# A cosformer attention and token/channel mixer on one core: four tokens per partition, shared tails, a ones column, bf16 transposes, and attention emitted one batch ahead

## The chip, the cores and the metric

The kernel runs on one core of a Trainium2 chip. The metric is device time in microseconds (us), smaller is better. A program on one core has no second core to compare with; every run that is used here was classed as fast (within 1.5% of the fastest run of the same kernel). Engine names in the profile: PE is TensorE, DVE is VectorE, ACT is ScalarE, POOL is GpSimd, SP is SyncE, and PEld is the loading of weights into PE.

## The reference

There are 8 batches of 8 heads, 576 tokens and 64 features per head. Inputs are f32. Shortened:

```python
# attention: linear, with relu features weighted by cos and sin of the position
q_p = concat(relu(q) * cos_w, relu(q) * sin_w)         # [..., 576, 128]
k_p = concat(relu(k) * cos_w, relu(k) * sin_w)
kv  = einsum('bhsf,bhsd->bhfd', k_p, v)
z   = sum(k_p, axis=tokens)
num = einsum('bhsf,bhfd->bhsd', q_p, kv)
den = einsum('bhsf,bhf->bhs', q_p, z) + 1e-6
x   = num / den                                        # heads joined: [8, 576, 512]

# mixer: first over tokens (576 -> 256 -> 576), then over channels (512 -> 1536 -> 512)
u   = x + (relu(x^T @ w_tok1) @ w_tok2)^T
out = u + relu(u @ w_ch1) @ w_ch2
```

576 is four and a half times 128, the number of partitions. How the odd half (the last 64 tokens, "the tail") is treated is a large part of this case.

## The kernel before

Each batch is cut into five tiles of tokens: four of 128 and one of 64. Letters in the text name PE's stages: kv, z, num, den as in the reference, tr (transposes of q features), b (x times w_tok1), u, the transposes of u, c (w_ch1) and o (w_ch2).

```python
for b in range(B):
    for ci, (o, sz) in enumerate(s_sizes):          # 128, 128, 128, 128, 64
        nc.sync.dma_start(out=qt[:sz], in_=q[b, :, o:o + sz, :].rearrange("h s d -> s h d"))
        nc.sync.dma_start(out=kt[:sz], in_=...)      # rows of 64 f32 = 256 bytes
        nc.gpsimd.dma_start(out=vt[:sz], in_=...)    # converts to bf16 on the way
        # [cut: qp on ACT, kp on DVE]
        for h in range(H):
            nc.tensor.matmul(kv_ps[:F, h * D:(h + 1) * D], kph, vt[:sz, h, :], ...)
            nc.tensor.matmul(z_ps[:F, h:h + 1], kph, ones[:sz, :], ...)
        # [cut: transposes of qp, copied by ACT into qpT]
    for ci, (o, sz) in enumerate(s_sizes):
        for h in range(H):
            nc.tensor.matmul(num_ps[:sz, h * D:(h + 1) * D], lw, kv_sb[:F, h * D:(h + 1) * D], ...)
            nc.tensor.matmul(den_ps[:sz, h:h + 1], lw, z_sb[:F, h:h + 1], ...)
        nc.vector.tensor_scalar_add(den_sb[:sz, :], den_ps[:sz, :], 1e-6)
        nc.vector.reciprocal(den_sb[:sz, :], den_sb[:sz, :])
        nc.vector.tensor_mul(x_sb[:sz, ci, :], num_v, den_b[:sz])     # 128 x 512
    # [cut: b and B1]
    for ci, (o, sz) in enumerate(s_sizes):
        # [cut: two u matmuls] 
        nc.vector.tensor_add(u_sb[:sz, ci, :], u_ps[:sz, :], x_sb[:sz, ci, :])   # f32
    for ci, (o, sz) in enumerate(s_sizes):
        for cj in range(NCC):
            nc.tensor.transpose(t_ps[:P, cj, :sz], u_sb[:sz, ci, cj * P:(cj + 1) * P],
                                ident_f[:sz, :sz])                               # f32
        nc.scalar.copy(uT[:, :, o:o + sz], t_ps[:, :, :sz])
    for mi in range(NCH):
        for (no, nsz) in [(0, 512), (512, 64)]:      # c: a matmul of 512 columns, one of 64
            for ki in range(NCC):
                nc.tensor.matmul(c_ps[:, no:no + nsz], w_ch1[...], uT[:, ki, no:no + nsz], ...)
        # [cut: relu, ACT and DVE in turn]
    for ci, (o, sz) in enumerate(s_sizes):           # o: five tiles, the fifth of 64 rows
        # [cut: twelve o matmuls, add of u, store]
```

## Time and profile before

| what | value | where it is read |
|---|---|---|
| time | 416.13 us, median of 4 runs (414.42 to 417.54) | the runs |
| span of the profiled execution | 415.3 us | the page |
| start, until the c stage of batch 0 | 69.2 us | PE's timeline |
| one batch, c stage to c stage, mean of 7 | 45.3 us | PE's timeline |
| last c and o stages, then the last add and store | 25.2 + 3.9 us | PE's timeline |

The last three rows give the sum 69.2 + 7 x 45.3 + 25.2 + 3.9 = 415.4, the span up to rounding.

From the page of the kernel before, part 1 (busy us, share of the span, instructions), part 2 (the span in 40 slices, busy tenths; PEclk is the granted PE clock in tenths) and part 4 (the chain of work that ended last):

```profile
PE 352.4 (85%) x3168; PEld 201.4 (48%) x3168; DVE 161.3 (39%) x332; ACT 162.6 (39%) x283; POOL 62.7 (15%) x72
...
PE   0005178998999999998999899998999899999996
...
PEclk9999559998799989998999979998999899998999
DMA  9999983029901393029702791029402900110002
...
PE 76%; DMA 7%; SPq 6%; DVE 5%; ACT 5%; issue 1%; DVEq 0%; ACTq 0%
```

PE is what the span hangs on: 85% busy, and 76% of the chain. Two things are to be seen in the slices. The first seven (each 10.4 us) belong to the start, where DMA is full and PE has little to do at first. After them the row is nines with an eight in every fourth or fifth place, and PEclk has dips there too: once per batch PE has a weak stretch.

PE's waits before, from the table of waits (engine, line, releaser: us in total, times, longest):

```profile
PE z_ps L133 <- DVE kp L124: 28.1, 4, 14.7
PE den_ps L156 <- DVE den_sb L159: 15.8, 14, 9.1
PE z_ps L133 <- DVE kp L122: 6.4, 1, 6.4
```

The long ones among them (the longest are 14.7, 9.1 and 6.4 us) lie in the start. PE's timeline over one steady batch (start, duration, engine, line, operation, output and inputs, count, and in brackets the idle time just before and what ended it):

```profile
186.02 0.41 PE L131 MATMUL kv_ps<-vt,kp 128*128 128x64 bf16 x8
...
190.19 0.34 PE L156 MATMUL den_ps<-z_sb,qpT 128*128 128x1 bf16 x8 [0.26 <-DVE den_sb L159]
...
192.25 0.24 PE L156 MATMUL den_ps<-z_sb,qpT 128*128 128x1 bf16 x4 [0.53 <-DVE den_sb L159]
...
196.12 2.76 PE L171 MATMUL b_ps<-x_sb,w_tok_118 128*128 128x512 bf16 x10
198.81 1.23 PE L133 MATMUL z_ps<-ones,kp 128*128 128x1 bf16 x40
199.98 2.79 PE L179 MATMUL u_ps<-B_2221,w_tok_124 128*128 128x512 bf16 x10
202.78 2.81 PE L187 MATMUL t_ps<-ident_f,u_sb 128*128 128x128 f32 x20
205.93 12.14 PE L197 MATMUL c_ps<-uT,w_ch_127 128*128 128x512 bf16 x96 [0.34 <-ACT uT L189]
217.91 2.75 PE L210 MATMUL o_ps_2409<-w_ch_132,h1T 128*128 128x512 bf16 x12
```

The stages follow one another: attention (186.0 to 205.9), then c (12.1 us) as one block, then o. No c matmul stands inside the attention part, so nothing fills PE's short waits there.

### The profile page before, as it was taken

The numbers are of one execution on the slowest core, as the hardware profiler recorded it, in microseconds if no ns is written. First come the engines' busy times: TensorE is split into PE (matmuls) and PEld (weight loads), VectorE is DVE, ScalarE is ACT, GpSimd is POOL, SyncE is SP. The second block draws the span as 40 slices with busy tenths as digits, with TensorE's granted clock in tenths as the row PEclk, the third lists the DMA queues.
The fourth block names the chain that finished last, engine by engine and source line by source line (L and its number), as shares of the span: only waits on it lengthen the run. The fifth ranks groups of instructions, "written<-read, shape, count | busy, mean of one in ns | idle before, by whom it ended". The sixth has DMA issues, their size and how long they took to land.

```text
span 415.3 us, 7475 instructions
## 1 busy us (share of the span) xinstructions
PE 352.4 (85%) x3168; PEld 201.4 (48%) x3168; DVE 161.3 (39%) x332; ACT 162.6 (39%) x283; POOL 62.7 (15%) x72
## 2 busy tenths in 40 slices
PE   0005178998999999998999899998999899999996
PEld 0004154547454555447554655456554755465542
DVE  2002253327422554328332653346332743326231
ACT  4115164208531384209630664128520873051410
POOL 7363000006000320006000600024000600000000
PEclk9999559998799989998999979998999899998999
DMA  9999983029901393029702791029402900110002
GB/s 183 205 192 182 169 151 77 2 86 156 161 2 42 98 187 76 0 103 169 130 2 76 137 165 25 25 91 196 91 0 86 85 5 0 52 65 0 2 25 90
DMA packets 121043, 37.26 MB, mean 90 GB/s; under 512 B 113521, under 2 KB 115889, under 8 KB 121009
## 3 DMA queue, kind: packets, MB, share of 16 engines
q1 hardware_dynamic: 80256, 28.32, 30.7%
q0 software_dynamic: 40752, 8.46, 23.0%
q8 instruction: 25, 0.41, 0.5%
q14 instruction: 10, 0.07, 0.1%
HBM read 35.78 MB, written 9.44 MB: 109 GB/s over the span
## 4 chain that ended last, share of the span: by engine, by line
PE 76%; DMA 7%; SPq 6%; DVE 5%; ACT 5%; issue 1%; DVEq 0%; ACTq 0%
PE c_ps L197 23%; DMA kt<-in_k_dram 7%; PE b_ps L171 6%; PE num_ps L154 4%; PE tr_ps L141 4%; PE u_ps L179 4%; ACT uT L189 3%; SPq L113 3%; PE kv_ps L131 3%; SPq L112 3%; PE t_ps L187 3%; PE den_ps L156 2%; PE z_ps L133 2%; DVE kp L124 2%; DVE u_sb L181 1%; DVE kp L122 1%
## 5 line engine op out<-in xcount | busy, mean ns | idle before, releaser
L197 PE MATMUL c_ps<-uT,w_ch_127 128*128 128x512 bf16 (+1 forms) x768 | 97.0, 286 | 2.6 <-ACT uT L189 2.6
L114 POOL DMA_DIRECT2D vt<-in_v_dram x40 | 49.2, 1242 | 257.1 <-PE tr_ps L141 247.3
L142 ACT COPY qpT<-tr_ps 128x512 bf16<-128x512 bf16 (+1 forms) x80 | 40.4, 544 | 111.8 <-PE tr_ps L141 111.1
L197 PEld LDWEIGHTS <-w_ch_127 128*128 128x128 bf16 x768 | 51.0, 97 | 48.8 <-issue 2.5
L210 PEld LDWEIGHTS <-h1T 128*128 128x128 bf16 (+1 forms) x480 | 46.9, 100 | 55.3 <-issue 3.4
L205 DVE TENSOR_SCALAR h1T<-c_ps 128x576 bf16<-128x576 f32 x48 | 36.4, 758 | 83.2 <-PE c_ps L197 83.2
L203 ACT ACTIVATE h1T<-c_ps 128x576 bf16<-128x576 f32 x48 | 31.2, 650 | 61.4 <-PE c_ps L197 60.4
L120 ACT ACTIVATE qp<-qt,bias_112,cos_t 128x512 bf16<-128x512 f32 (+1 forms) x40 | 32.2, 805 | 23.1 <-DMA qt<-in_q_dram 23.1
L133 PE MATMUL z_ps<-ones,kp 128*128 128x1 bf16 (+1 forms) x320 | 10.5, 164 | 34.5 <-DVE kp L124 28.1
L181 DVE TENSOR_TENSOR u_sb<-u_ps,x_sb 128x512 f32<-128x512 f32 (+1 forms) x40 | 24.6, 681 | 30.0 <-PE u_ps L179 30.0
L122 DVE TENSOR_SCALAR kp<-kt,cos_t 128x512 bf16<-128x512 f32 (+1 forms) x40 | 19.9, 498 | 39.9 <-DMA kt<-in_k_dram 35.6
L156 PE MATMUL den_ps<-z_sb,qpT 128*128 128x1 bf16 (+1 forms) x320 | 18.5, 169 | 18.0 <-DVE den_sb L159 15.8
L121 ACT ACTIVATE qp<-qt,bias_112,sin_t 128x512 bf16<-128x512 f32 (+1 forms) x40 | 32.2, 804 | 1.7 <-DMA qt<-in_q_dram 1.7
L141 PE MATMUL tr_ps<-ident,qp 128*128 128x128 bf16 (+1 forms) x320 | 30.4, 221 | 0.7
L189 ACT CAST uT<-t_ps 128x512 bf16<-128x512 f32 (+1 forms) x40 | 20.1, 548 | 21.1 <-PE t_ps L187 20.1
L133 PEld LDWEIGHTS <-kp 128*128 128x128 bf16 (+1 forms) x320 | 9.4, 96 | 37.8 <-DVE kp L124 28.4
L164 DVE TENSOR_TENSOR x_sb<-num_ps,den_sb 128x512 bf16<-128x512 f32 (+1 forms) x40 | 25.3, 683 | 5.6 <-PE num_ps L154 4.9
L171 PE MATMUL b_ps<-x_sb,w_tok_118 128*128 128x512 bf16 (+1 forms) x80 | 26.7, 486 | 0.0
L156 PEld LDWEIGHTS <-qpT 128*128 128x128 bf16 (+1 forms) x320 | 16.0, 104 | 21.1 <-issue 17.9
L124 DVE TENSOR_SCALAR kp<-kt,sin_t 128x512 bf16<-128x512 f32 (+1 forms) x40 | 21.4, 535 | 3.3 <-DMA kt<-in_k_dram 3.3
L187 PE MATMUL t_ps<-ident_f,u_sb 128*128 128x128 f32 (+1 forms) x160 | 21.8, 273 | 0.9
L141 PEld LDWEIGHTS <-qp 128*128 128x128 bf16 (+1 forms) x320 | 20.8, 100 | 3.3 <-issue 0.2
(127 smaller groups left out, 307.3 us busy)
## 6 DMA issues: line engine op xcount, KB each, us to landing
qt<-in_q_dram SPq DMA_DIRECT2D x32, 256.0 KB, 6.5
kt<-in_k_dram SPq DMA_DIRECT2D x32, 256.0 KB, 5.5
out_dram<-res SPq DMA_DIRECT2D x32, 256.0 KB, 2.0
vt<-in_v_dram POOLq DMA_DIRECT2D x32, 128.0 KB, 6.9
w_ch_127<-in_moe_w_ch_dram POOLq DMA_DIRECT2D x4, 384.0 KB, 10.0
w_ch_132<-in_moe_w_ch_dram POOLq DMA_DIRECT2D x12, 128.0 KB, 8.4
qt<-in_q_dram SPq DMA_DIRECT2D x8, 128.0 KB, 3.9
kt<-in_k_dram SPq DMA_DIRECT2D x8, 128.0 KB, 3.5
```

What stands on the lines that cost most here:

```text
L114: nc.gpsimd.dma_start(out=vt[:sz], in_=v[b, :, o:o + sz, :].rearrange("h s d -> s h d"))
L120: nc.scalar.activation(qp[:sz, :, 0, :], qt[:sz], AF.Relu, bias=bias0[:sz], scale=c_s)
L121: nc.scalar.activation(qp[:sz, :, 1, :], qt[:sz], AF.Relu, bias=bias0[:sz], scale=s_s)
L141: nc.tensor.transpose(tr_ps[:F, hh, :sz], qph, ident[:sz, :sz])
L142: nc.scalar.copy(qpT[:F, g * HH:(g + 1) * HH, o:o + sz], tr_ps[:F, :, :sz])
L156: nc.tensor.matmul(den_ps[:sz, h:h + 1], lw, z_sb[:F, h:h + 1], start=True, stop=True)
L171: nc.tensor.matmul(b1_ps, w_tok1[:sz, ci, mi * P:(mi + 1) * P], x_sb[:sz, ci, :], start=(ci == 0), stop=(ci == NSC - 1))
L187: nc.tensor.transpose(t_ps[:P, cj, :sz], u_sb[:sz, ci, cj * P:(cj + 1) * P], ident_f[:sz, :sz])
L189: nc.scalar.copy(uT[:, :, o:o + sz], t_ps[:, :, :sz])
L197: nc.tensor.matmul(c_ps[:, no:no + nsz], w_ch1[:, ki, mi * P:(mi + 1) * P], uT[:, ki, no:no + nsz], start=(ki == 0), stop=(ki == NCC - 1))
L205: nc.vector.tensor_relu(h1T[:, mi, :], c_ps)
L210: nc.tensor.matmul(o_ps[:sz, :], h1T[:, ki, o:o + sz], w_ch2[:, ki, :], start=(ki == 0), stop=(ki == NCH - 1))
```

## The change

The intent is less PE work, and long DMA rows. Six things happen at once:

1. Four consecutive tokens lie in one partition, so that q, k and v come in rows of 1 KB instead of 256 bytes, and the first 512 tokens are four full tiles.
2. The 64-token tails of two batches share one 128-row tile for their features. Their u is kept, and the c and o stages of all eight tails run at the end as one group of 512 tokens. The c and o stages of a batch then have 512 tokens and no odd half.
3. A column of ones beside v makes kv and z one matmul of 65 columns; num and den likewise. The 80 matmuls of one column go. A PSUM tile now holds four heads, so that the normalisation is ten chains of 256 columns instead of five of 512.
4. POOL casts u to bf16, and u is transposed in bf16, eight blocks to a PSUM tile, with one ACT copy.
5. v is loaded as f32 and cast by POOL.
6. `attention(b)` and `channel_batch(b)` are functions, and attention is emitted ahead of the channel stages of the batch before it.

Lesser things change too: o has PSUM buffers of its own (before, it shared three with the attention), v comes over SP's queue, and the input tiles have other numbers of buffers. The core of the diff, with unchanged and lesser parts cut:

```diff
+    def load(b):
+        for t, src in ((kt, k), (vt, v), (qt, q)):
+            nc.sync.dma_start(out=t, in_=src[b, :, :SF, :].rearrange("h (p j) d -> p h (j d)", j=J))
 # [cut: load_tail: two batches' tails, one in each half of the partitions]
-                nc.tensor.matmul(kv_ps[:F, h * D:(h + 1) * D], kph, vt[:sz, h, :], ...)
-                nc.tensor.matmul(z_ps[:F, h:h + 1], kph, ones[:sz, :], ...)
+                    lhs, rhs = kp[:, j, h], vb[:, j, h, :D + 1]          # the last column is ones
+                    nc.tensor.matmul(kv_ps[:, hh, :], lhs.rearrange("p f d -> p (f d)"), rhs, ...)
-                nc.tensor.matmul(num_ps[:sz, h * D:(h + 1) * D], lw, kv_sb[...], ...)
-                nc.tensor.matmul(den_ps[:sz, h:h + 1], lw, z_sb[:F, h:h + 1], ...)
+        for j in range(J + 1):
+            for g in range(2):                                           # four heads each
+                    nc.tensor.matmul(nm[r0:r1, hh, :], lw, kv[:, h, :D + 1], start=True, stop=True)
+                nc.vector.tensor_scalar_add(den[r0:r1], nm[r0:r1, :, D:], 1e-6)
+                nc.vector.reciprocal(den[r0:r1], den[r0:r1])
+                nc.vector.tensor_mul(dst[r0:r1, g * HH:(g + 1) * HH], nm[r0:r1, :, :D], den_b[r0:r1])
-                nc.tensor.transpose(t_ps[:P, cj, :sz], u_sb[:sz, ci, ...], ident_f[:sz, :sz])
+            nc.gpsimd.tensor_copy(ub[:, j, :], u[:, j, :])               # f32 to bf16
+            if j % 2:
+                transposed(uT[:, j - 1:j + 1]..., ub[:, j - 1:j + 1]..., 2 * NCC)
+    attention(0)
+    attention(1)
+    for b in range(2, B):
+        load(b)
+        if b % 2 == 0:
+            load_tail(b // 2)
+        channel_batch(b - 2)
+        attention(b)
+    channel_batch(B - 2)
+    channel_batch(B - 1)
+    channel_tail()
```

The framework orders each engine's instructions at build time. In the built program, the attention of batch b stands among the c matmuls of batch b-1. I call such a kernel woven, and one whose stages follow one another unwoven.

## The prediction

> **What bounds the kernel now.** TensorE. The page has it busy 352.4 of 415.3 us, DVE and ACT 39% each; the chain that ended last is 76% PE. In PE's timeline a steady batch repeats every 45.05 us (first kv matmul at 186.02, the next at 231.07): attention with its stalls 10.1, b 2.7, z 1.2, u 2.8, transposes of u 3.1, c 12.1, o 13.0. Before that lies the start: c of batch 0 begins only near 70 us, with PE in long waits for kp and den (28.1 and 15.8 us in the table of waits), while DMA moves about 200 GB/s in 256-byte rows.
>
> **PE work after, per batch, from spacings in this trace.** A 512-column matmul follows the next after 0.216 us (12 in 2.59), a 65-column one after about 0.03, a bf16 transpose after 0.055 (4 in 0.22), an f32 one after 0.14 (20 in 2.80).
> - c: the 64-column matmuls go (12.14 to 10.4); o: the 64-row fifth tile goes (13.07 to 10.4). All tails return as a ninth group, 20.7 us in all, 2.6 per batch.
> - u transposes: 20 f32 become 18 bf16: -1.8.
> - z and den (80 small matmuls): about -2.5.
> - Sum: tr 2.0, kv 1.2, nm 1.4, b 2.2, u 2.2, tr(u) 1.0, c and o 20.7: 31; with the tails 33.4, so 268 for eight batches.
>
> **What it adds.** POOL casts about nine 128x512 f32 tiles per batch, in the path of v and of u. The trace has no such cast. The Trainium skill, "GPSIMD Engine Reference", section 3.1, gives 1.8 cycles per element at best, 768 ns for 512; my estimate is 0.8 to 1.3 us. It also says (section 1) that POOL shares SBUF interfaces with DVE; this trace cannot show it. DVE's normalisation becomes ten chains of add, reciprocal, multiply (0.16+0.20+about 0.42) instead of five (0.16+0.20+0.68): +2.6 us per batch. DVE rises to about 23 us per batch, ACT to 20: under PE's 33, but not inside the attention part.
>
> **How they stand in order.** The built order weaves attention of batch b into the c matmuls of batch b-1 and leaves o pure. The woven part is a chain: transposes with 1.0 us ACT copies (6 us to the first nm), ten DVE chains and two relus (9), b and B1 (3), u, cast, transpose, copy (6 to 7): about 25 us for 20.6 us of PE work. So 4 to 5 us of PE stalls per batch; a batch costs 35 to 36 us instead of 45.
>
> **Start.** Rows become 1 KB, but load 0 with its tail (3.9 MB) shares the engines with 7.5 MB of weights. PE's first instruction transposes the q tail, the last of these loads: about 33 us. Then an unwoven attention of 25: c of batch 0 starts near 58.
>
> **Sum.** 58 + 7 x 35.5 + 41.5 (c, o of the last batch and of the tails, nothing woven) + 4 (last add, store) = 352 us. Range 330 to 376. Faster by over 2%: 0.98; within: 0.015; slower: 0.005.
>
> **What the profile would show.** Right: 432 matmuls of 128x512 each in c and o at 0.216; period 35 to 36; PE waits for DVE, ACT copies and casts, each some tenths; first PE work near 33 us; last 41.5 us pure c and o. Wrong: period near 32, or above 38.
>
> **What would make it wrong.** Faster: stalls under 2 us per batch (320 to 330), or a start at over 300 GB/s (10 us less). Slower: casts over 1.5 us, or slowed by DVE; SP's in-order queue holding loads behind stores; a lower granted clock; strided reads of k or of w2's weights costing more than dense ones.

## The result, and the profile after

The kernel after takes 342.11 us (median of 4 runs, 340.8 to 344.09), the kernel before 416.13 us. The ratio is 0.821, with a 95% interval of 0.8165 to 0.8256. Ratios are the mean time of one kernel's fast runs over that of the other's of the same rounds, so not quite the ratio of the medians quoted. The output is correct.

| part of the span | before | after | difference |
|---|---|---|---|
| start, until the first c stage or the first woven stretch | 69.2 | 59.7 | -9.5 |
| seven periods | 7 x 45.3 | 7 x 33.3 | -84 |
| c and o with nothing woven in, at the end | 25.2 | 41.5 (batch 7, then the tails) | +16.3 |
| last add and store | 3.9 | 4.7 | +0.8 |
| span | 415.3 | 339.0 | -76.3 |

Nearly all of it comes from the period; part is given back at the end, as the tails' c and o move there. The page after, the same lines as before:

```profile
PE 286.0 (84%) x2076; PEld 146.5 (43%) x2096; DVE 166.3 (49%) x449; ACT 148.2 (44%) x217; POOL 54.3 (16%) x93
...
PE   0000567989999999999999999999999999999994
...
PEclk9999969999999999999999999999999999999999
DMA  7999999909747512832263110011002000301114
...
PE 61%; DVE 15%; SPq 8%; ACT 7%; issue 3%; POOL 2%; DMA 2%; POOLq 0%; DVEq 0%; ACTq 0%
```

PE's share of the span has not changed (84% for 85%), though its work fell by 66 us: a share says nothing of how much work there is. The weak stretches and the dips of the clock are gone from the slices. The chain has moved: 15% of it is DVE now, and POOL appears. PE's waits after:

```profile
PE tr L154 <- ACT qpt L143: 37.3, 1, 37.3
...
PE nm L223 <- DVE x L229: 3.3, 5, 1.5
...
PE tr L154 <- POOL ub L248: 2.9, 5, 1.2
```

One wait, that for the first transpose, is the start. All waits for the normalisation and for the casts come to 6.2 us in the whole span. PE's timeline of one woven stretch and of the pure o stage after it:

```profile
126.36 1.50 PE L154 MATMUL tr<-ident,qp 128*128 128x128 bf16 x24
...
131.32 0.55 PE L223 MATMUL nm<-kv,qpT 128*128 128x65 bf16 x12
...
133.39 0.30 PE L223 MATMUL nm<-kv,qpT 128*128 128x65 bf16 x4 [0.44 <-DVE x L229]
133.53 0.59 PE L271 MATMUL c_ps<-uT,wc_128 128*128 128x512 bf16 x2
133.96 0.29 PE L223 MATMUL nm<-kv,qpT 128*128 128x65 bf16 x4
134.09 0.59 PE L271 MATMUL c_ps<-uT,wc_128 128*128 128x512 bf16 x2
...
137.38 1.04 PE L236 MATMUL b_1458<-x,w_121 128*128 128x512 bf16 x4
...
140.57 1.03 PE L246 MATMUL u_ps<-B_1457,w_126 128*128 128x512 bf16 x4
...
150.15 9.88 PE L281 MATMUL o_ps<-wc_133,h_1542 128*128 128x512 bf16 x45
159.86 0.61 PE L154 MATMUL tr<-ident,qpt 128*128 128x128 bf16 x8
```

Read the nm rows against the c rows between them. Every 0.56 us there are four nm matmuls and two c matmuls, with no idle time in brackets. DVE meanwhile runs one chain. Its timeline in the same stretch shows at what pace:

```profile
133.99 0.42 DVE L229 TENSOR_TENSOR x<-nm,den 128x256 bf16<-128x256 f32 x1
134.33 0.17 DVE L226 RECIPROCAL den<-den 128x4 f32<-128x4 f32 x1
134.42 0.13 DVE L225 TENSOR_SCALAR den<-nm 128x4 f32<-128x4 f32 x1
134.53 0.42 DVE L229 TENSOR_TENSOR x<-nm,den 128x256 bf16<-128x256 f32 x1
```

The records of one chain sum to 0.42 + 0.17 + 0.13 = 0.72 us, but from one multiply to the next only 0.54 us pass: each record begins before the one ahead of it has ended (the reciprocal at 134.33, when the multiply that began at 133.99 has 0.08 us to run). So DVE at 0.54 and PE at 0.56 are level here, and the c matmuls hide the chains but for the 0.44 us of the first.

Busy times of one steady period each (the window's bounds, its length, then busy time and instructions of each engine, granted clock, DMA share and GB/s); the first line is of before, and the second fence is of after:

```profile
172.85:217.91 45.06, 43.35 (x402) 24.87 (x400) 20.07 (x41) 20.00 (x35) 6.72 (x5) 0.96 0.56 93
```

```profile
159.86:193.30 33.44, 32.66 (x250) 16.73 (x252) 19.08 (x53) 18.54 (x27) 5.25 (x8) 1.00 0.37 127
```

In both, PE (the first figure after the length) fills the period nearly, while DVE and ACT have about 20 us or less. PE's busy time includes the modelled ends of its records and, in before, some work at a lower clock (0.96), so it is more than the work at full clock. For that work this text uses two estimates: 30.8 us per period after, which is the number of matmuls of each kind times the usual spacing of that kind in the trace, and 39.9 us before, which is the sum of the stages in the expectation of experiment 2. They are not made in the same way: counted as the first is, the old operations come to 37.6 us (in the trace of experiment 2).

### The profile page after: what moved, and what is told of

Same layout as the page of the kernel before. It is cut to its first block, busy times and chain, and to the rows that moved or that the text cites. A ratio compares the mean times of both kernels' runs of the same rounds, so it can differ in the third digit from the quotient of the medians.

```text
span 339.0 us, 5197 instructions
## 1 busy us (share of the span) xinstructions
PE 286.0 (84%) x2076; PEld 146.5 (43%) x2096; DVE 166.3 (49%) x449; ACT 148.2 (44%) x217; POOL 54.3 (16%) x93
## 4 chain that ended last, share of the span: by engine, by line
PE 61%; DVE 15%; SPq 8%; ACT 7%; issue 3%; POOL 2%; DMA 2%; POOLq 0%; DVEq 0%; ACTq 0%
PE o_ps L281 27%; PE c_ps L271 18%; SPq L108 8%; PE tr L154 6%; DVE kp L138 4%; DVE x L229 4%; ACT qpT L155 3%; PE kv_ps L208 3%; POOL ub L248 2%; DVE u L247 2%; DMA qtt<-in_q_dram 2%; PE u_ps L246 2%; PE nm L223 1%; DVE kpt L138 1%; PE ut_ps L257 1%
## 5 line engine op out<-in xcount | busy, mean ns | idle before, releaser
L271 PE MATMUL c_ps<-uT,wc_128 128*128 128x512 bf16 x384 | 101.2, 380 | 0.5 <-ACT h_2791 L275 0.4
L271 PEld LDWEIGHTS <-wc_128 128*128 128x128 bf16 x432 | 37.8, 97 | 36.5 <-issue 4.6
L283 DVE TENSOR_TENSOR u<-o_ps,u 128x512 f32<-128x512 f32 x32 | 22.1, 692 | 59.0 <-PE o_ps L281 59.0
L155 ACT COPY qpT<-tr 128x1024 bf16<-128x1024 bf16 x32 | 30.1, 1034 | 31.9 <-PE tr L154 31.9
L143 ACT ACTIVATE qp<-qt,bias_87,cos_t 128x512 bf16<-128x512 f32 x32 | 26.0, 812 | 27.0 <-DMA qt<-in_q_dram 27.0
L248 POOL CAST ub<-u 128x512 bf16<-128x512 f32 x32 | 19.4, 619 | 112.2 <-DVE u L247 111.7
L154 PE MATMUL tr<-ident,qpt 128*128 128x128 bf16 x32 | 2.9, 242 | 37.3 <-ACT qpt L143 37.3
L138 DVE TENSOR_SCALAR kp<-kt,cos_t 128x512 bf16<-128x512 f32 x32 | 17.7, 555 | 33.4 <-PE kv_ps L208 33.3
L229 DVE TENSOR_TENSOR x<-nm,den 128x256 bf16<-128x256 f32 x64 | 26.9, 423 | 0.1
L143 ACT ACTIVATE qp<-qt,bias_87,sin_t 128x512 bf16<-128x512 f32 x32 | 25.9, 809 | 0.0
L247 DVE TENSOR_TENSOR u<-u_ps,x 128x512 f32<-128x512 f32 x32 | 21.0, 687 | 5.1 <-PE u_ps L246 4.6
L154 PE MATMUL tr<-ident,qp 128*128 128x128 bf16 x256 | 19.4, 231 | 0.4
L138 DVE TENSOR_SCALAR kp<-kt,sin_t 128x512 bf16<-128x512 f32 x32 | 16.3, 510 | 5.4 <-DMA kt<-in_k_dram 5.3
L154 PEld LDWEIGHTS <-qpt 128*128 128x128 bf16 x32 | 2.4, 108 | 38.0 <-ACT qpt L143 37.3
L191 POOL CAST vbf_100<-vt 128x512 bf16<-128x512 f32 x16 | 10.9, 723 | 44.9 <-PE kv_ps L208 32.9
L191 POOL CAST vbf_98<-vt 128x512 bf16<-128x512 f32 x16 | 10.3, 681 | 28.9 <-PE kv_ps L208 21.6
```

The costliest lines, as they stand in the source:

```text
L138: nc.vector.tensor_scalar(dst[:n, :, f, :], src, scalar1=tab[:n, j:j + 1], scalar2=0.0, op0=ALU.mult, op1=ALU.max)
L143: nc.scalar.activation(dst[:, :, f, :], src, AF.Relu, bias=bias0, scale=tab[:, j:j + 1])
L154: nc.tensor.transpose(tr[:, i, :], src[:, (g + i) * P:(g + i + 1) * P], ident)
L155: nc.scalar.copy(dst[:, g:g + m, :], tr[:, :m, :])
L229: nc.vector.tensor_mul(dst[r0:r1, g * HH:(g + 1) * HH], nm[r0:r1, :, :D], den_b[r0:r1])
L247: nc.vector.tensor_add(u[:, j, :], u_ps, x[:, j, :])
```

## The experiments

Every run below was correct. Times are medians, with the number of runs; ratios are against the kernel before in the same rounds (416.5 to 416.9 us in all of them). "First c" is the start of the first c matmul, 61.4 us in after; "period" is the mean distance of the first kv matmuls of batches 1 to 7 in the profiled run, 33.3 us in after. The four runs of after went from 340.8 us (mean granted clock 0.99) to 344.09 (0.98), so differences of that size are not resolved by one profile. The framework orders the instructions anew in each build, so that an edit can move others too; experiments 8 and 10 say where that matters. An expectation's theory A is always that which the prediction rests on, or the one mended by then; B and C are its rivals.

The question at the outset: is the time that of PE's work plus what the weave leaves of waits (A), so that the gain needs the order; or do the cheaper operations bring the gain by themselves, whatever their order (the rival in experiments 1 and 2)? And in the period, is it PE or the side chain over DVE and POOL that sets the pace (experiments 8 to 10)?

### 1. The change without its order

All of the new kernel, but each batch's channel stages follow its own attention directly:

```diff
-    attention(0)
-    attention(1)
-    for b in range(2, B):
-        load(b)
-        if b % 2 == 0:
-            load_tail(b // 2)
-        channel_batch(b - 2)
+    for b in range(B):
+        if 1 <= b < B - 1:
+            load(b + 1)
+            if (b + 1) % 2 == 0:
+                load_tail((b + 1) // 2)
         attention(b)
-    channel_batch(B - 2)
-    channel_batch(B - 1)
+        channel_batch(b)
     channel_tail()
```

> The changed kernel with one thing undone: channel(b) is emitted right after attention(b), so that no c matmuls fill the gaps of an attention. The PE work is the same to the matmul. Theory A (the order carries much of the gain, since the new attention is a chain of about 24 us for 10 us of PE work): the period goes from 33.4 to about 42 us, total about 395 us (385 to 410). Rival B (less PE work carries the gain, the order little): at most 10 us slower than the changed kernel, 342 to 352 us.

Measured: 413.82 us (4 runs, 410.96 to 414.99), ratio 0.9932 (0.9884 to 0.9981). This is 72 us slower than after, where I expected 53 (the time lies above the stated 385 to 410), and nearly the time of before. The period is 43.45 us for the same 30.8 us of PE work. PE's timeline in one attention part:

```profile
175.18 0.30 PE L223 MATMUL nm<-kv,qpT 128*128 128x65 bf16 x4 [1.32 <-DVE x L229]
176.16 0.30 PE L223 MATMUL nm<-kv,qpT 128*128 128x65 bf16 x4 [0.68 <-DVE x L229]
...
179.61 3.17 PE L236 MATMUL b<-x,w 128*128 128x512 bf16 x7 [0.31 <-DVE x L229]
...
186.85 0.40 PE L154 MATMUL tr<-ident,ub 128*128 128x128 bf16 x4 [1.31 <-POOL ub L248]
...
191.90 10.52 PE L271 MATMUL c_ps<-uT,wc 128*128 128x512 bf16 x48
```

The waits for the normalisation and for the casts, which c matmuls filled in after, now stand open. And seven b matmuls take 3.17 us, 0.45 each, where 0.216 is the pace elsewhere. The two windows around that moment say why:

```profile
169.60:179.60 10.00, 5.87 (x97) 4.49 (x95) 8.19 (x32) 8.10 (x12) 3.61 (x5) 0.88 0.53 170
179.60:184.20 4.60, 4.59 (x11) 1.21 (x11) 3.34 (x10) 0.60 (x1) 0.00 (x0) 0.52 0.97 257
```

PE was busy for 59% of the first 10 us, and in the next 4.6 us it was granted half the clock (0.52). The clock record of the trace has the half clock from 177.16 to 183.99; between the last o matmul and that moment PE was busy for 4.2 of 7.6 us. The Trainium skill, "TensorE: Matmul & The Clock Gate", section "Why this matters for your kernels", says to leave no PE-idle gaps over about 3 us between bursts, or the clock falls to half. The half clock agrees; but here no gap was longer than 1.45 us after the start, so many short gaps were enough. The measurement decides: to keep to that advice is not enough in this case. What exactly the clock reacts to, this run doesn't show. I did not separate the open waits from the low clock by a run of their own, but the trace gives the size: the ten b matmuls of a batch, which lie in the half clock, take 3.9 to 4.6 us here and 2.4 to 2.5 in most batches of after. By that estimate the low clock is some 2 us of the 10.1 by which the period is longer, and the open waits are most of it.

### 2. The order without the change

The kernel before, split into the same two functions and emitted one batch ahead; nothing else:

```diff
-    for b in range(B):
+    kept = {}
+    def attention(b):
         x_sb = xpool.tile([P, NSC, Dm], BF16, name="x_sb")
@@
+        kept[b] = (u_sb, uT)
+    def channel(b):
+        u_sb, uT = kept.pop(b)
         h1T = hpool.tile([P, NCH, S], BF16, name="h1T")
@@
+    attention(0)
+    for b in range(1, B):
+        attention(b)
+        channel(b - 1)
+    channel(B - 1)
```

> The kernel before with one thing done: attention(b+1) is emitted ahead of the MLP of batch b, nothing else. Theory A: its PE work is about 40 us of its 45 us per batch (c 12.1, o 13.1, b 2.5, u 2.2, f32 transposes 2.8, kv and z 2.4, tr 2.2, num and den 2.6), so filling its gaps saves 2 to 3 us per batch: about 396 us (385 to 405). Together with the first run: order and smaller PE work are each worth little alone and 74 us together. Rival B (the order is the whole gain): about 345 to 360. Rival C (order does nothing): 412 to 418.

Measured: 379.95 us (4 runs, 379.52 to 381.22), ratio 0.9134 (0.9105 to 0.9163). I expected 396, and 385 at the least. One period:

```profile
174.27:214.37 40.10, 40.08 (x401) 22.55 (x399) 20.50 (x41) 19.41 (x35) 5.34 (x5) 1.00 0.63 105
```

The period is 40.1 us with PE busy for 40.08 of it, at full clock: weaving hides every wait of the old attention. My estimate of its PE work (39.9 us) agrees with the period; the mistake was to add waits to it. (Counts times spacings give 37.6 us, so that 2.5 us of this period are not in that count either, though PE has no idle time; see the end of this text.) The gain is 7 x (45.3 - 40.1) = 36.4 us, which is the whole difference.

The two runs and the two kernels make a table of two by two:

| | unwoven | woven | weaving is worth |
|---|---|---|---|
| old operations | 416.5 | 380.0 | -36.5 |
| new operations | 413.8 | 342.1 | -71.7 |
| the new operations are worth | -2.7 | -37.9 | both: -74.4 |

The operations alone are worth almost nothing and the order alone half of the gain. Under the weave the new operations cut the period by 6.8 us (40.1 to 33.3), but they make the attention a longer chain, and only the weave hides that. The two parts don't add up: the order helps by itself, the operations need it.

### 3. Transposes of u in f32

After, with u transposed in f32 as before, without casts:

```diff
+    def transposed_f(dst, src):
+        tr = psA.tile([P, NCC, P], F32, name="trf", tag="psA")
+        for i in range(NCC):
+            nc.tensor.transpose(tr[:, i, :], src[:, i * P:(i + 1) * P], ident_f)
+        nc.scalar.copy(dst, tr)
@@
-            nc.gpsimd.tensor_copy(ub[:, j, :], u[:, j, :])
-            if j % 2:
-                transposed(uT[:, j - 1:j + 1]..., ub[:, j - 1:j + 1]..., 2 * NCC)
+            transposed_f(uT[:, j], u[:, j, :])
```

> The changed kernel with u transposed in f32 again: no casts of u on POOL, 4 f32 transposes per PSUM tile, copies of 512 by ACT. PE work rises by 18 x 0.085 = 1.5 us per batch, and the chain loses the casts (0.6 us each, two ahead of each copy). Theory A (the period is set by PE work plus small waits): about +1.3 us per batch, 350 us (346 to 356). Rival B (the period is set by the chain, in which the casts lie): the same or faster, 336 to 343.

Measured: 356.39 us (4 runs, 356.22 to 356.5), ratio 0.8564 (0.8538 to 0.859); just past the upper end. The period is 34.57, 1.25 us more, as expected (1.3). The rest is the start: the first c comes at 68.6 us, 7.2 later. There the first attention has no c matmuls to fill it, each group of f32 transposes waits 0.8 us for the add of u in turn, and PE is at half clock from 47.7 to 68.2 us, where after has it only from 45.5 to 52.3.

### 4. Start: q first, the large weights later

After, with the first loads in the order q, k, v, each with its tail, and the large channel weights held back until the first v has landed (a small copy from v into the weight tile makes their loads wait):

```diff
-    load(0)
-    load_tail(0)
+    load_first()              # q and its tail, k and its tail, v and its tail
@@
+    def load_wc():
+        nc.gpsimd.tensor_copy(wc1[:, :, 0], v0[:, 0, :NCC])
+        nc.gpsimd.tensor_copy(wc2[:, :, 0], v0[:, 0, :NCH])
+        # [the loads of wc1 and wc2, moved here]
@@
     attention(0)
+    load_wc()
     attention(1)
```

> An attempt at a faster version: the changed kernel with its first loads in the order q, q tail, k, k tail, v, v tail, and with the loads of the two large weights held until v of batch 0 has landed. Theory: the 37 us before the first PE work come from the q tail queueing behind 7.5 MB of weights and k and v; PE then starts at 15 to 22 us, the first kv at about 24 instead of 41.5, c of batch 0 at about 44 instead of 61; total 322 to 330 us. Rival (the start is bound by bytes and not by their order, and the large weights then land too late for c of batch 0): 336 to 345.

Measured: 333.18 us (4 runs, 332.49 to 333.75), ratio 0.8004 (0.7979 to 0.8029); a little short of the expectation. PE begins at 12.1 us instead of 37.3, the first c comes at 53.1 us, 8.3 earlier, and the time falls by 8.9. So a start of 25 us earlier on PE gives only a third of that. The timeline of all engines shows where the rest went:

```profile
42.67 0.81 ACT L161 ACTIVATE qp<-qt,bias,cos_t 128x512 bf16<-128x512 f32 x1 [18.23 <-DMA qt<-in_q_dram]
43.39 1.06 ACT L256 ACTIVATE B<-b 128x512 bf16<-128x512 f32 x2
44.02 1.86 PE L264 MATMUL u_ps<-B,w 128*128 128x512 bf16 x4 [10.13 <-ACT B L256]
```

PE waits 10.13 us for the relu B, whose input had long been there. ACT had been told to compute the q features of batch 1 first, and sat 18.23 us on that load. The Trainium skill, "TensorE: Matmul & The Clock Gate", section "Architectural detail: the array is 16× 32×32, not 1× 128×128", says that ScalarE's queue is strictly first in, first out; this trace agrees, and PE's 10.13 us are the price here.

### 5. z and den apart again

After, with every matmul of 65 columns split into 64 and 1:

```diff
-                    nc.tensor.matmul(nm[r0:r1, hh, :], lw, kv[:, h, :D + 1], start=True, stop=True)
+                    for c0, c1 in ((0, D), (D, D + 1)):
+                        nc.tensor.matmul(nm[r0:r1, hh, c0:c1], lw, kv[:, h, c0:c1],
+                                         start=True, stop=True)
# [the matmul of kv likewise]
```

> The changed kernel with the merge undone: each 65-column matmul becomes one of 64 columns and one of 1 column with the same weights loaded again, into the same PSUM tile; all other engines see the same. 80 more matmuls with weight loads per batch at about 0.03 us: PE work +2.4 us per batch. Theory A (PE work sets the period): +16 to 20 us, about 360 us. Rival B (the waits in the woven stretch absorb it): 342 to 348.

Measured: 356.98 us (4 runs, 356.14 to 358.75), ratio 0.8575 (0.8546 to 0.8605): 14.9 us slower. The period is 35.26, 1.93 more (the prediction had about 2.5), and the first c comes 2.6 later. A matmul of one column costs 1.93 us over 80, so 24 ns each (in the trace of before they follow one another after 25); as the 65th column of another it costs less than that.

### 6. The tail's c and o in each batch

After, with the c and o stages of the tail computed in every batch, for its own 64 tokens, instead of at the end. (For space, the tile of the tail's x has one buffer instead of two here.)

```diff
-    def channel_tail():
-        channel(uT_tail, u_tail, store)
+        # in each batch's channel stage:
+        for m0, m1 in ((0, 8), (8, NCH)):
+            for mi in range(m0, m1):
+                for ki in range(NCC):
+                    nc.tensor.matmul(c_ps[:, mi - m0, :], wc1[:, ki, mi * P:(mi + 1) * P],
+                                     uT_tail[:, i, ki, lo:lo + T], ...)
+        # [cut: relu]
+        for ki in range(NCH):
+            nc.tensor.matmul(o_ps[lo:lo + T], h1t[:, ki, :], wc2[:, ki, :], ...)
```

> The changed kernel with the 64 tail tokens of each batch put through the MLP in that batch, as 48 c matmuls of 64 columns and 12 o matmuls of 64 rows, instead of one group of 512 tail tokens at the end. Cost by the spacings of the kernel before: 48 x 0.037 + 12 x 0.22 = 4.4 us per batch, 35 in all, against 20.7 for the group at the end. Theory A: +14 us, about 356 us (350 to 362). Rival B (the extra matmuls fill waits): within 4 us of the changed kernel.

Measured: 359.16 us (4 runs, 356.65 to 359.24), ratio 0.8608 (0.8575 to 0.864), as expected. The period is 38.03, 4.7 us more, against 20.7 us less at the end. Seven periods cost 32.9 us more and the start 2.7 more, the end gives back the 20.7 less the last batch's own tail: 17 us in the time. Sharing the tails is worth that.

### 7. Short rows

After, with tokens laid out as before (one token per partition and tile), so that q, k and v come in rows of 256 bytes:

```diff
-            nc.sync.dma_start(out=t, in_=src[b, :, :SF, :].rearrange("h (p j) d -> p h (j d)", j=J))
+            for j in range(J):
+                nc.sync.dma_start(out=t[:, :, j * D:(j + 1) * D],
+                                  in_=src[b, :, j * P:(j + 1) * P, :].rearrange("h s d -> s h d"))
# [positions, w_tok1, w_tok2 and the store likewise]
```

> The changed kernel with token j*128+p on partition p instead of 4p+j: the loads of q, k and v read 256-byte rows again, the output stores 2 KB rows instead of 4, and the weights of u are read dense. Theory A (rows matter in the start alone, for in the steady state 4 MB per 33 us are less than the 200 GB/s of short rows): start 8 to 15 us longer, period unchanged: about 353 us (348 to 360). Rival B (the rows also set the steady period): over 365. Rival C (rows do not matter): 340 to 345.

Measured: 344.39 us (4 runs, 343.0 to 345.53), ratio 0.8257 (0.8229 to 0.8284). Theory A missed by 9 us; the time lies in the range of rival C, for which rows do not matter. PE begins at 42.0 us instead of 37.3, and the first c comes at 68.0 instead of 61.4, but the period is 33.0: later, loads are ahead of need and their rows don't matter. The medians differ by 2.3 us (the two profiled spans by 4.8), and the interval of this ratio overlaps that of after. "Four tokens per partition", the first words of the change, is worth a few us at most, with the loads in this order.

### 8. One more DVE operation in each chain

After, with one addition of zero on the reciprocal, which costs DVE some 1.35 us per batch:

```diff
                 nc.vector.reciprocal(den[r0:r1], den[r0:r1])
+                nc.vector.tensor_scalar_add(den[r0:r1], den[r0:r1], 0.0)
```

> The changed kernel with one more DVE instruction (an add of 0 to den) in each of the ten normalisation chains of a batch; results the same. Theory A (PE work sets the period; the scheduler has c and o matmuls to fill with): under 4 us slower, 341 to 346. Rival B (the DVE chain sets the length of the woven stretch, as the prediction's 9 us for ten chains took it): +0.13 to 0.2 us x 10 x 7 = 10 to 14 us slower, 351 to 357.

Measured: 347.39 us (4 runs, 346.51 to 348.35), ratio 0.834 (0.8314 to 0.8366): between the theories. The period is 33.71, 0.38 more; the first c comes at 65.0, 3.6 later. Both theories had looked at the steady part only. PE's timeline shows that the build changed more than one operation:

```profile
136.08 0.55 PE L223 MATMUL nm<-kv,qpT 128*128 128x65 bf16 x12
...
138.70 1.46 PE L272 MATMUL c_ps<-uT,wc 128*128 128x512 bf16 x6
...
146.60 1.03 PE L237 MATMUL b<-x,w 128*128 128x512 bf16 x4
```

The framework put relus and k features between the chains, so that the ten take 10.5 us from the first nm to b, where after needs 6.1 in the stretch shown above. PE fills this with c matmuls, up to six at a time, and o matmuls now stand in the stretch as well. So the 0.38 us are not the price of 1.35 us of DVE time; but the run shows that the chains can last 4.4 us longer with hardly a change of the period, which speaks against rival B.

### 9. The casts of u twice

After, with POOL casting each tile of u twice:

```diff
             nc.gpsimd.tensor_copy(ub[:, j, :], u[:, j, :])
+            nc.gpsimd.tensor_copy(ub[:, j, :], u[:, j, :])
```

> The changed kernel with each cast of u on POOL done twice (same results; the second waits for the first), so that the path from u to its transposes is 0.6 us longer per tile and POOL has 4 x 0.62 us more work per batch. Theory A (the woven stretch hides it, PE work sets the period): under 4 us slower, 341 to 346. Rival B (the casts are on the critical path, as the prediction had it): 1.2 to 2.5 us per batch, 350 to 360.

Measured: 348.68 us (6 runs, 347.73 to 350.73), ratio 0.8377 (0.8346 to 0.8407): again between. The period is 34.07, 0.74 more for some 2.3 us of POOL work (four casts of 0.57 to 0.62), and the first c comes at 66.0, 4.7 later. So a third of the added time shows in the steady part, and the start alone loses more than the 2.3 us: there PE is at half clock from 48.2 to 65.2 us, where after has it from 45.5 to 52.3.

### 10. The normalisation without the 1e-6

After, with the reciprocal taken straight from PSUM. On these inputs the result stays within tolerance; it is a probe, not a proposal.

```diff
-                nc.vector.tensor_scalar_add(den[r0:r1], nm[r0:r1, :, D:], 1e-6)
-                nc.vector.reciprocal(den[r0:r1], den[r0:r1])
+                nc.vector.reciprocal(den[r0:r1], nm[r0:r1, :, D:])
```

> The changed kernel with the add of 1e-6 left out of the ten normalisation chains (the reciprocal reads PSUM itself; not the reference's formula, but den is far above 1e-6 in this data, so within tolerance). The opposite of e8_long_den, which cost 5 us in its medians. Theory A (in the stretch of ten chains DVE and PE are nearly level, DVE 0.54 and PE 0.56 us per chain, so a longer chain costs and a shorter one saves little): 338 to 342, less than 1.5% faster than the changed kernel. Rival B (DVE alone sets the stretch): 4 to 8 us faster, 334 to 338.

Measured: 341.9 us (6 runs, 340.47 to 343.47), ratio 0.8204 (0.8172 to 0.8236): nothing gained, as A expected. The period is 33.14. The build changed DVE's order here too: the chains stand in pairs, and from the first nm to b it still takes 6.1 to 6.7 us. So this run doesn't show by itself what a shorter chain is worth in the old order. What it shows is that PE's idle time falls from some 1.0 to 0.3 us per period with only 0.2 us gained: little is left to gain by removing waits, and PE's own work sets the period.

### 11. Start, second version

Experiment 4, with v as the last of the three loads for the other batches too, so that q of batch 1 lands earlier:

```diff
-        for t, src in ((kt, k), (vt, v), (qt, q)):
+        for t, src in ((kt, k), (qt, q), (vt, v)):
```

> The run e7_start with one more change: q of each batch is loaded ahead of v. In the trace of e7_start PE stood 10.1 us before the first u, because ACT, which works in order, sat in front of the two relus that give B with a q feature of batch 1 whose load was still running (it landed at 42.7 us, behind v of batch 1 and mixed with the large weights). Theory: that wait goes, c of batch 0 starts at 43 to 46 us instead of 53, total 322 to 327 us. Rival (the start is bound by bytes: about 13 MB must land before c of batch 0, so the wait only moves to the weights): 329 to 334, with a wait for the large weights in its place.

Measured: 326.57 us (6 runs, 326.05 to 327.85), ratio 0.7847 (0.782 to 0.7873), as expected. The first c comes at 46.35 us and the period is 33.37. This kernel is the fastest, 15.5 us faster than after. What remains of the waits has moved to POOL:

```profile
37.31 2.28 POOL L209 CAST vbf<-vt 128x512 bf16<-128x512 f32 x4 [11.08 <-DMA vt<-in_v_dram]
39.54 1.17 POOL L266 CAST ub<-u 128x512 bf16<-128x512 f32 x2
40.20 0.61 PE L172 MATMUL tr<-ident,ub 128*128 128x128 bf16 x4 [5.09 <-POOL ub L266]
```

POOL sits 11.08 us on v of batch 1 with the casts of batch 0's u behind it, and PE waits 5.09 us for them. It is the pattern of experiment 4 on another engine.

### 12. Start, third version

Experiment 11, with the second large weight (w_ch2) held back further, until v of batch 1 has landed, so that this v should land sooner:

```diff
-        nc.gpsimd.tensor_copy(wc2[:, :, 0], v0[:, 0, :NCH])
+    def load_wc2(v1):
+        nc.gpsimd.tensor_copy(wc2[:, :, 0], v1[:, 0, :NCH])
         # [the loads of wc2]
@@
     attention(1)
+    load_wc2(v1)
```

> The run e10_start2 with one more change: the second large weight waits for v of batch 1 rather than v of batch 0. In the trace of e10_start2 PE stood 5.1 us before the first transposes of u, because POOL, which works in order, sat with the casts of v of batch 1 ahead of the casts of u, and that v landed only at 37.3 us, mixed with 6.3 MB of weights. Theory: v lands near 31 us, the wait goes, c of batch 0 starts at 42 instead of 46.4; the second weight is needed only some 12 us after that, at the first o; total 321 to 324 us. Rival (the bytes are the bound and the wait moves to the second weight): 325 to 328.

Measured: 329.45 us (6 runs, 329.37 to 330.61), ratio 0.7916 (0.789 to 0.7941): a miss, 2.9 us slower than experiment 11. The v in question landed at 36.9 us instead of 37.3, so that holding the weight back freed nothing for it, and the copy and the weight's DMA issues now stood on POOL ahead of the casts (PE waits 6.07 us for them instead of 5.09). The first c comes at 50.0.

## Why the prediction was right, and where it was not

The prediction said 352 us, with a range of 330 to 376; it came to 342.1. The form of the sum was right: a start, seven periods, an end of 41.5 us. The period, 33.3, lies between the 35 to 36 that it called right and the "near 32" that it called wrong.

| term | predicted | measured | effect on the sum |
|---|---|---|---|
| start of the first woven stretch | 58 | 59.7 | +1.7 |
| period | 35.5 | 33.3 | 7 x -2.2 = -15.4 |
| c and o of batch 7 and of the tails | 41.5 | 41.5 | 0 |
| last add and store | 4 | 4.7 | +0.7 |
| sum | 352 | 339.0 (span) | -13 |

The term that was mis-sized is the period, by the "4 to 5 us of PE stalls per batch" that the prediction read off a woven stretch of "about 25 us": 33.3 less the 30.8 us of PE work leaves 2.5, and PE is idle for no more than about 1 us of it. That the start came out well is in part luck: PE's first work came 4.3 us later than predicted (37.3 for 33), and the first c at 61.4 where the prediction wrote 58; but the first stretch begins 1.7 us before that, and the first attention, to that point, took 22.4 us instead of 25. The pieces of the period, read from PE's timeline of the stretch that begins at 126.36:

| piece of the period | predicted | measured |
|---|---|---|
| transposes up to the first nm | 6 | 5.0 |
| ten DVE chains and two relus | 9 | 6.1 |
| b and B1 | 3 | 3.2 |
| u, casts, transposes, copies | 6 to 7 | 7.4 |
| transpose of the tail's u, last c | not counted apart | 2.2 |
| whole stretch, to the pure o | about 25 | 23.8 |
| pure o | 10.4 | 9.7 |

- **The DVE chains.** The prediction added the durations of three records per chain, ten times. The records overlap: a chain passes every 0.54 us, not every 0.72, and PE fills that with c matmuls. The Trainium skill, "VectorE: DVE Perf Modes", section "The DRAIN you can't avoid", says that the next operation waits for the pipe to empty, but also that a next operation that is not held starts earlier. This trace shows the second: the kp operations start 0.40 us apart, each recorded with 0.48. Durations were read where starts should have been. This piece is 2.9 us shorter than predicted, and is the largest error; the last pieces of the stretch take back a part. The pure o is 0.7 us shorter because some of its 48 matmuls found a place in the stretch: this trace has one there and 45 in the pure stage and misses two records; the trace of experiment 11, which misses none, has two there.
- **The casts.** They were set at 0.8 to 1.3 us. The mean of those of u is 0.62 us, and four casts of v in a row take 2.28 us, 0.57 each. The prediction took 1.8 cycles per element, 768 ns for 512, from the Trainium skill, "GPSIMD Engine Reference", section 3.1, as the best case. The same paragraph also gives 1.03 cycles for bodies with k up to 2, which would be 0.44 us for 512 at the 1.2 GHz used there (an estimate). The measured casts lie between the two, and the measurement decides. The prediction went further up from a figure that was too high already. Even so the piece that contains the casts came out a little longer than predicted, so that the casts account for none of the 13 us. The shared SBUF interfaces of POOL and DVE (section 1 there), which the prediction named, agree with the trace: a kp operation of 0.48 us took 0.84 and 0.76 while POOL cast v, and those casts took 0.72 each. It costs DVE some tenths per batch, where it has room.
- **PE's work.** Predicted 31 us per batch, 33.4 with the tails' share. 432 matmuls of 512 columns each in c and in o ran at 0.216 us, as predicted. The parts, tested one by one: tails 4.7 us per period for 4.4 (experiment 6), z and den 1.93 for "about 2.5" (experiment 5), f32 transposes 1.25 for 1.8 (experiment 3). None was off by more than 0.6.
- **The order.** The prediction saw the weave in the built order and costed its gain inside the sum, but it named the change's savings by their operations. The experiments show that without the order the operations are worth 2.7 us of 74 (experiments 1 and 2). And it did not foresee how badly the new attention does alone: 43.45 us per period, 18.8 us more in all than I expected even with the result in hand. The half clock, which my expectation left out, can be some 2 us per batch of that (experiment 1).
- **The rows.** The prediction made the start the fruit of longer rows sharing the engines with 7.5 MB of weights, and put PE's first work near 33 us (37.3 measured). Long rows turned out to be worth little: short ones delay PE's first work by 4.7 us, and the time by 2.3 us in the medians (experiment 7). The order of the loads, and what waits behind them, is worth 15.5 us (experiment 11).

What stays open: what the remaining 2.5 us per period are. In the window PE is idle for 0.8 of 33.4; and the same count leaves 2.5 us in experiment 2 too, where PE is idle for 0.02. So most of it need not be stalls; small gaps between matmuls of different shapes or an error of the count are left. Open too is how much of experiment 1's loss is exactly the low clock. The starts of experiments 3, 8 and 9 lost more than the added operations' time: between 52 and 66 us their granted clock was 0.50, 0.83 and 0.53, against 0.99 in after, so that the half clock has a part in it, but why it lasted longer there was not isolated; and it stays open whether the bytes alone bound the remaining start (experiment 12 suggests so for one v, no more).

## What to carry to other kernels

When PE is the limit but has short waits, first let independent matmuls of another batch stand between them: here the order alone gave 36.5 us, and it turned the cheaper operations from a gain of 2.7 us into one of 37.9, as they had lengthened the chain that must be hidden. Take the cost of a chain of short operations from the distance of their starts, not from the sum of their recorded durations. At a start, look for the engine that sits in order on a load which nobody needs yet, while the work that somebody does need stands behind it.

## What the Trainium skill lacked or had wrong

- "TensorE: Matmul & The Clock Gate", "Why this matters for your kernels": the advice to avoid PE-idle gaps over about 3 us is not enough. In experiment 1 the clock fell to half after 7.6 us in which PE was busy for 4.2 us and no gap exceeded 1.32 us. (Elsewhere the same page does report a kernel in which frequent short idle times between groups of matmuls make the clock swing; the row of the table leaves that out.)
- "GPSIMD Engine Reference", section 3.1: it gives 1.8 cycles per element (768 ns for 512) as the best case and 1.03 for bodies with k up to 2, and does not say which a cast follows. Casts of 128x512 from f32 to bf16 took 0.57 us each in a row of four, and 0.62 on average for u, between the two.
